# Attention's output by groups of 32 rows, and the state's update by heads, in a kernel of attention and two mixtures

## The chip, the core and the metric

The kernel runs on one core of one Trainium2 chip. The metric is the time of one execution on the device, in microseconds (us). A core has five engines that run at the same time, each through its own instructions in order: TensorE (PE in the profile; its loads of stationary operands are listed apart as PEld), VectorE (DVE), ScalarE (ACT), GpSimd (POOL) and SyncE (SP), which here issues most transfers. TensorE writes its products into PSUM, which has eight banks here.

## The reference

Three stages follow each other. The first is a recurrent attention over 768 steps, for 4 batches of 8 heads with 48 features each. The second is a mixture with a softmax gate on each hidden value over 3072 tokens of 384 features, and the third sends each token to one of 8 experts.

```python
for t in range(S):                       # attention: B, H, S, D = 4, 8, 768, 48
    cur = np.einsum('bhd,bhe->bhde', u[None] * kt, vt)
    y[:, :, t] = np.einsum('bhd,bhde->bhe', rt, state + cur)
    state = wt[:, :, :, None] * state + np.einsum('bhd,bhe->bhde', kt, vt)
x = attn_out.transpose(0, 2, 1, 3).reshape(B * S, H * D)
h = x @ w_in                             # 384 -> 1024
solu = h * softmax(h)
x = layernorm(solu) * g_ln @ w_out       # 1024 -> 384
e = argmax(x @ w_gate, axis=1)           # one of 8 experts for each token
out = gate * (relu(x @ w1[e]) @ w2[e])
```

## The kernel before

The 768 steps of a batch are cut into 6 chunks of 128, so that attention is 24 units of work (one chunk of one batch, 128 tokens by 384 features). In a unit the 8 heads form 4 pairs, p = 0 to 3, with q = 0 or 1 for the head in the pair. The state of a batch, `St[b]`, has for each pair 128 rows (64 for each head, 48 of them used) and 96 columns (48 for each head); blocks off the diagonal are zero.

A unit does this. TensorE transposes the inputs `lw`, `lr`, `lk` (line 693); DVE runs the decay's products along the chunk (line 709). The scores of each head (line 767) are products over 48 rows. They lie in rows 0 to 47 for q = 0 and 64 to 111 for q = 1, and go to bank 4 and bank 5; DVE copies them under the causal mask into `am` (line 771). Then comes the output, `y()`, at line 780. It is written transposed, features on the partitions, into bank 4: for each pair one product of the state's 96 columns with `rt` (none in a batch's first chunk), and for each head one product of 96 columns of `lv` with `am[:, q, p]`. In `lv` each head has 48 columns of values and 48 of zeros, so that a window of 96 columns puts a head's values into its half of the pair's 96 rows. The result has 96 partitions and 4 blocks of 128 tokens.

The mixture's weights are multiplied in three blocks of 128 features. So `high()` and `low()` (lines 785 to 793) copy the output into `xh` and `xl` as three blocks of 128 rows: rows 0 to 95 are pairs 0 to 2, and rows 96 to 127 hold a third of pair 3 each. That is four copies on ACT (line 785, and line 787 three times) and four subtractions on DVE (line 791, and line 793 three times). `x_rows` gives the rows of `w_in` the same order, which makes two transfers of each of the six loads of `w_in`.

The state's update multiplies the transposed keys `ks` (128 stationary columns of a pair) with the values of both heads (96 moving columns) at line 810; DVE adds the state (line 818) and POOL multiplies the diagonal blocks by the decay (line 823). In the middle stretch its product, the output and the scores of q = 0 share bank 4, one after the other.

All operands of lines 767, 780 and 810 are float32. Where the built program has one such product, the trace shows two instructions on PE; this text calls them passes. The mixture's products (lines 187 to 190) take operands split in two and are one instruction each.

The order is written out by hand. Each step has a nominal time, and a table of numbers says in which order the steps are issued; every engine keeps that order. First, attention runs beside the preparation of the mixture's weights (until some 116 us). Then attention's unit s runs beside the mixture's tile s - 7 (until some 376 us); the last seven tiles and the experts follow. Products that nobody reads (`warm`, line 1087) fill PE at some places of the first stretch.

Of the kernel before, what the change touches and what calls it, by code (L numbers as in the profile page):

```python
# [7 lines left out]
F32 = mybir.dt.float32  # L8
# [5 lines left out]
ALU = mybir.AluOpType  # L14
# [17 lines left out]
# Places by number of tokens, in the order in which they are worked on, and the room of each; the last one's rest has a path of its own.  # L32
# [5 lines left out]
# Issue order: position in the issue sequence -> index of the step in the plan sorted by nominal time.  # L38
# [82 lines left out]
def rwkv_moe_kernel(ctx: ExitStack, tc: tile.TileContext, r, k, v, w, u, w_in, w_out, g_ln, w_gate, w1, w2, out, dbg=None):  # L121
# [44 lines left out]
    # sums of the inverse decay products, of the squares of the first mixture, of the decay products: bounds that NaN fails too  # L166
# [16 lines left out]
    def mm3(o, terms):  # L183
        """The products of operands in two parts each, high parts first; the product of both low ones is below float32."""
        n = len(terms)
        for i, (ah, al, bh, bl) in enumerate(terms):
            nc.tensor.matmul(o, ah, bh, start=(i == 0), stop=False)  # L187
            nc.tensor.matmul(o, ah, bl, start=False, stop=False)  # L188
        for i, (ah, al, bh, bl) in enumerate(terms):
            nc.tensor.matmul(o, al, bh, start=False, stop=(i == n - 1))  # L190

    def mm3_steps(o, terms, n):
        """The same in pieces of n products."""
        seq = [(ah, b) for ah, al, bh, bl in terms for b in (bh, bl)] + [(al, bh) for ah, al, bh, bl in terms]
        for i, (a, b) in enumerate(seq):
            nc.tensor.matmul(o, a, b, start=(i == 0), stop=(i == len(seq) - 1))  # L196
            if i % n == n - 1:
                yield
# [5 lines left out]
    # A plan is a list of steps with nominal times; every engine issues its steps in that order.  # L204
# [11 lines left out]
    # The rows of a block of the attention's transpose: those of a pair of heads, and a third of the last pair's.  # L216
    def x_rows(kk):
        return (slice(0, 96), slice(96 * kk, 96 * kk + 96)), (slice(96, 128), slice(3 * 96 + 32 * kk, 3 * 96 + 32 * kk + 32))

    def from_f64(src, n, pool, ck=None):  # L220
        """float64 to float32 by its bits: sign and exponent and 20 bits of the high word, 3 of the low one.
        Below float32's range it is 0, or, with ck, sums there say that a value was below."""
# [21 lines left out]
    def prep_w_in(c, pool, ck=None):  # L244
        kk, n = divmod(c, 2)
        ns = slice(512 * n, 512 * n + 512)
        a = yield from from_f64([(rows, w_in[at, ns]) for rows, at in x_rows(kk)], 512, pool, ck)
        yield lambda: nc.scalar.copy(out=wih[:, kk, ns], in_=a)
        yield lambda: nc.gpsimd.tensor_tensor(out=wil[:, kk, ns], in0=a, in1=wih[:, kk, ns].bitcast(F32), op=ALU.subtract)
# [7 lines left out]
    def prep_gate(f, st, wgt, pool, tp, gp):  # L257
        """Rows of w_out times the gate's weights, for the logits to come out of the same product as the mixture."""
        def tr():
            for kk in range(KD):  # L260
                nc.tensor.transpose(tp[:, kk, :], st()[:, kk * 128:(kk + 1) * 128], ident)
        yield tr
        wT = pool("wT")[:, 0:DM].rearrange("p (k n) -> p k n", k=KD)
        yield lambda: nc.scalar.copy(out=wT, in_=tp)

        def lg():
            for kk in range(KD):
                nc.tensor.matmul(gp[:, f, :], wT[:, kk, :], wgt[:, kk, :], start=(kk == 0), stop=(kk == KD - 1))
        yield lg
# [43 lines left out]
    def moe_act(u, halves, mw):  # L313
        """halves: the hidden values, as one pattern or as two of one bank each."""
# [121 lines left out]
    def experts_loop(x2d=None, tokd=None):  # L436
        """Every expert over all tokens, the others' results dropped; without those over its sorted rows."""
# [56 lines left out]
    def general_path():  # L494
# [44 lines left out]
        with ExitStack() as gs:  # L539
# [11 lines left out]
            with tc.For_i(0, NTOK, 128) as t0:  # L551
                x = ga2.tile([128, DM], F32, tag="gx", name="gx")
                xk = x.rearrange("p (k n) -> p k n", k=KD)
                nc.sync.dma_start(out=xk[:, :, 0:96], in_=xd[bass.ds(t0, 128), 0:288].rearrange("p (k n) -> p k n", k=KD))
                nc.sync.dma_start(out=xk[:, :, 96:128], in_=xd[bass.ds(t0, 128), 288:384].rearrange("p (k n) -> p k n", k=KD))
# [20 lines left out]
    # the attention's buffers go when its last tile is done, and those of the experts take their room  # L576
# [23 lines left out]
    def xslot(m):  # L600
        """Where the two parts of a tile's transpose wait: in the first weight buffers, as long as no expert has them; one place apart, for the last tile."""
# [15 lines left out]
    def lazy(t, make, gaps):  # L617
        """Steps of a generator that allocates as it goes: each is drawn when its turn comes."""
# [10 lines left out]
    # Nominal times of the steps of a unit from the start of its step: attention with the preparation of  # L629
    # w_out beside it, with that of w_in, with a tile of the mixture, and the mixture alone.  # L630
# [122 lines left out]
    def plan_A(i, t, mode):  # L753
# [5 lines left out]
        yp = bank[4][0:2 * D]  # L759
# [15 lines left out]
        def y():  # L775
            vf = v_.rearrange("p h d -> p (h d)")
            terms = [(p, St[b][:, p, :], u["rt"][:, p, :]) for p in range(4)] if c else []
            terms += [(p, vf[:, 96 * (2 * p + q) - 48 * q:96 * (2 * p + q) - 48 * q + 96], u["am"][:, q, p, :]) for q in range(2) for p in range(4)]
            for n, (p, a, m) in enumerate(terms):
                nc.tensor.matmul(yp[:, p, :], a, m, start=(n == 0), stop=(n == len(terms) - 1), skip_group_check=True)  # L780
# [3 lines left out]
        def high():  # L784
            nc.scalar.copy(out=xh[0:96], in_=yp[:, 0:3, :])
            for kk in range(KD):
                nc.scalar.copy(out=xh[96:128, kk, :], in_=yp[32 * kk:32 * kk + 32, 3, :])
        at(o("x"), high)

        def low():  # L790
            nc.vector.tensor_tensor(out=xl[0:96], in0=yp[:, 0:3, :], in1=xh[0:96].bitcast(F32), op=ALU.subtract)
            for kk in range(KD):
                nc.vector.tensor_tensor(out=xl[96:128, kk, :], in0=yp[32 * kk:32 * kk + 32, 3, :], in1=xh[96:128, kk, :].bitcast(F32), op=ALU.subtract)
# [14 lines left out]
        def mm():  # L808
            for p in range(4):
                nc.tensor.matmul(up[:, p, :].rearrange("p (q d) -> p q d", q=2), u["ks"][:, p, :], v_[:, 2 * p:2 * p + 2, 0:D], start=True, stop=True)  # L810
# [40 lines left out]
    # groups of token tiles that are gated together  # L851
# [44 lines left out]
    def gate_steps(g, bk):  # L896
        """The first of the largest logits' experts, its gate, the row among the sorted tokens, and the way there."""
# [69 lines left out]
    # The first is the one with most of the first tokens, so that its work can start before the last tokens have theirs;  # L967
    # the others follow by their numbers of tokens, as PLACE has it. The j-th has room for SLOTS[j] tokens.
# [90 lines left out]
    # the first loads, then the constant buffers  # L1059
# [8 lines left out]
    def init():  # L1068
# [10 lines left out]
        # each partition's sums start at its share of the expert's first row: ranks come out as rows  # L1079
# [4 lines left out]
    def warm(n):  # L1084
        """The tensor engine's clock rises only under load: products that nobody reads, where there is no work yet."""
# [21 lines left out]
    def scratch(c):  # L1107
        """Where the preparation of a block of weights works: buffers that the mixture uses later."""
# [12 lines left out]
    def named(make, times):  # L1121
        """Steps of a generator at given times."""
# [80 lines left out]
    def check():  # L1203
        """1 for more tokens of the last place, 2 for a place with too little room, 4 for decays or values out of bounds or an expert's rows overrun."""
# [79 lines left out]
    # the first expert's first tokens, beside the end of the first mixture  # L1284
# [18 lines left out]
    # the order of the others  # L1303
# [18 lines left out]
    for j in range(1, NE):  # L1322
        # the weights and tokens of a place are made ready during the one before
# [72 lines left out]
```

## Time and profile before

| | |
|---|---|
| median of 3 runs | 702.67 us (701.42, 702.67, 703.84) |
| profiled execution, from its first to its last instruction | 701.8 us |
| PE busy | 650.1 us (93%), 4279 instructions |
| DVE, ACT, POOL busy | 444.6, 346.1, 350.8 us |
| mean granted clock of PE | 0.972 of 2.4 GHz |

For the profiled execution the page gives the span alone; its own time on the device is not listed apart from the three runs. A matmul's end is modelled in the profile, so that matmuls in a row overlap on paper: how long one occupies PE is read from the distance between starts. A "busy" PE can therefore be waiting for its own pipeline.

### The profile page before, as it was taken

The page shows a single profiled execution, that of the slowest core. Times are in us where ns is not written, and L with a number is a line of the kernel's source. Part 1 is how long each engine was busy: PE and PEld are TensorE (multiplying, and loading weights), DVE is VectorE, ACT ScalarE, POOL GpSimd, SP SyncE. Part 2 cuts the span into 40 slices and gives each one's busy share as a digit, 9 for nine tenths or more (in the row PEclk, how much of TensorE's full clock was granted, in tenths as well). Part 3 has the DMA queues.
Part 4 walks back from the last instruction along what each step waited for, and adds up shares of the span by engine and source line. Part 5 has one row for each costly group of instructions (what it writes and reads, how often), then busy time and mean ns, then how long its engine had stood idle before and what let it go on. Part 6 is the DMA issues. An engine that isn't in the chain of part 4 may idle for free. (4 is left out here: it accounts for less than half of the span.)

```text
span 701.8 us, 11888 instructions
## 1 busy us (share of the span) xinstructions
PE 650.1 (93%) x4279; PEld 604.1 (86%) x4279; DVE 444.6 (63%) x947; ACT 346.1 (49%) x759; POOL 350.8 (50%) x341
## 2 busy tenths in 40 slices
PE   6787779898999999999989999999999999999993
PEld 6777668887988978998978998999899999999993
DVE  7999999968987888699887779752203121131220
ACT  3677566545553545545643556433535344353430
POOL 5666578344344445344461153326637374667721
PEclk9789799999999999999999999999999999999997
DMA  7856323562611413050200420155444253544400
GB/s 175 210 132 146 95 59 90 170 170 58 147 35 33 104 23 68 23 114 24 57 35 13 154 84 13 57 160 188 149 141 139 91 176 125 182 135 145 157 20 35
DMA packets 125193, 72.45 MB, mean 103 GB/s; under 512 B 104167, under 2 KB 115932, under 8 KB 125125
## 3 DMA queue, kind: packets, MB, share of 16 engines
q1 hardware_dynamic: 121845, 62.13, 33.3%
q0 software_dynamic: 3280, 9.47, 3.6%
q8 instruction: 36, 0.59, 0.4%
q14 instruction: 32, 0.26, 0.1%
HBM read 55.79 MB, written 16.29 MB: 103 GB/s over the span
## 5 line engine op out<-in xcount | busy, mean ns | idle before, releaser
L1257 DVE SCALAR_TENSOR_TENSOR hl<-bank,hh 128x384 fp32r<-128x384 f32 (+5 forms) x70 | 37.6, 552 | 141.4 <-ACT hh L1256 125.8
L1050 POOL TENSOR_TENSOR wbl<-stg,wbh 128x768 fp32r<-128x768 f32 x32 | 58.8, 1852 | 30.0 <-ACT wbh L1049 25.6
L196 PE MATMUL bank<-wbh,hh 128*128 128x384 f32 (+4 forms) x216 | 72.9, 338 | 0.0
L196 PE MATMUL bank<-wbl,hh 128*128 128x384 f32 (+4 forms) x216 | 72.6, 336 | 0.0
L187 PE MATMUL bank<-xth,wah 128*128 128x384 f32 (+5 forms) x210 | 71.2, 345 | 0.5 <-DVE rr L955 0.5
L1050 POOL TENSOR_TENSOR wal<-stg,wah 128x1024 fp32r<-128x1024 f32 x24 | 57.3, 2401 | 28.1 <-ACT wah L1049 28.1
L188 PE MATMUL bank<-xtl,wah 128*128 128x384 f32 (+5 forms) x210 | 69.7, 337 | 0.0
L187 PE MATMUL bank<-wbh,lh 128*128 128x392 f32 x192 | 67.5, 351 | 1.3 <-ACT xo L873 0.8
L1256 ACT ACTIVATE hh<-bank 128x384 fp32r<-128x384 f32 (+5 forms) x70 | 33.6, 490 | 66.6 <-PE bank L190 59.0
L188 PE MATMUL bank<-wbl,lh 128*128 128x392 f32 x192 | 65.5, 341 | 0.0
L748 POOL TENSOR_TENSOR am<-ident,a 128x1024 f32<-128x1024 f32 x24 | 46.7, 1946 | 28.0 <-DVE a L743 19.8
L1276 POOL DMA_INDIRECT out_dram<-yo,xg x28 | 27.6, 984 | 64.6 <-ACT yo L1273 42.7
L726 POOL TENSOR_TENSOR tq<-qe,yq 128x512 f32<-128x512 f32 x24 | 29.7, 1238 | 60.0 <-ACT yq L721 59.9
L780 PE MATMUL bank<-am,lv 128*96 128x128 f32 x384 | 49.3, 284 | 5.7 <-DVE am L771 4.8
L780 PEld LDWEIGHTS bank<-am,lv 128*96 128x96 f32 x384 | 45.9, 171 | 6.7 <-DVE am L771 3.2
L823 POOL TENSOR_TENSOR St<-su,qe 64x192 f32<-64x192 f32 x40 | 24.8, 621 | 48.0 <-DVE su L818 36.4
L190 PE MATMUL bank<-xth,wal 128*128 128x384 f32 (+5 forms) x210 | 48.2, 337 | 0.0
L961 POOL DMA_INDIRECT xsd<-xo,ai x24 | 25.4, 1057 | 35.0 <-DMA xsd<-xo,ai 14.1
L187 PE MATMUL pair<-wah,wah 128*128 128x512 f32 x102 | 42.1, 413 | 0.0
L196 PE MATMUL bank<-wbh,hl 128*128 128x384 f32 (+4 forms) x216 | 42.1, 336 | 0.0
L187 PEld LDWEIGHTS bank<-xth,wah 128*128 128x128 f32 x210 | 39.5, 188 | 2.3 <-DVE rr L955 0.7
L188 PEld LDWEIGHTS bank<-xtl,wah 128*128 128x128 f32 x210 | 39.5, 188 | 1.3
(241 smaller groups left out, 1753.0 us busy)
## 6 DMA issues: line engine op xcount, KB each, us to landing
stg<-in_moe_w_dram SPq DMA_DIRECT2D x32, 384.0 KB, 4.5
stg<-in_moe_w_dram SPq DMA_DIRECT2D x24, 512.0 KB, 4.5
xsd<-zrow SPq DMA_DIRECT2D x16, 386.0 KB, 3.8
xg<-xsd SPq DMA_DIRECT2D x24, 193.0 KB, 2.7
lw<-in_w_dram SPq DMA_DIRECT2D x24, 192.0 KB, 3.3
lr<-in_r_dram SPq DMA_DIRECT2D x24, 192.0 KB, 4.2
lk<-in_k_dram SPq DMA_DIRECT2D x24, 192.0 KB, 3.8
lv<-in_v_dram SPq DMA_DIRECT2D x24, 192.0 KB, 3.1
```

The costliest lines, as they stand in the source:

```text
L187: nc.tensor.matmul(o, ah, bh, start=(i == 0), stop=False)
L188: nc.tensor.matmul(o, ah, bl, start=False, stop=False)
L190: nc.tensor.matmul(o, al, bh, start=False, stop=(i == n - 1))
L196: nc.tensor.matmul(o, a, b, start=(i == 0), stop=(i == len(seq) - 1))
L726: nc.gpsimd.tensor_tensor(out=u["tq"], in0=u["qe"][:, :, 1:129], in1=u["yq"], op=ALU.mult)
L748: nc.gpsimd.tensor_tensor(out=u["am"].rearrange("p q a t -> p (q a) t"), in0=ident.rearrange("p (o t) -> p o t", o=1).to_broadcast([128, H ...
L780: nc.tensor.matmul(yp[:, p, :], a, m, start=(n == 0), stop=(n == len(terms) - 1), skip_group_check=True)
L961: nc.gpsimd.indirect_dma_start(out=xsd, out_offset=bass.IndirectOffsetOnAxis(ap=u["ai"][:, j, :], axis=0), in_=MU[m]["xo"], in_offset=None ...
L1050: at(t + c1, lambda: eng.tensor_tensor(out=dl(), in0=u["st"], in1=dh().bitcast(F32), op=ALU.subtract))
L1256: at(t + d1, lambda: nc.scalar.activation(out=P2["h", 0][:, f, cs], in_=hp, func=AF.Relu))
L1257: at(t + d2, lambda: nc.vector.scalar_tensor_tensor(out=P2["h", 1][:, f, cs], in0=hp, scalar=0.0, in1=P2["h", 0][:, f, cs].bitcast(F32), o ...
L1276: nc.gpsimd.indirect_dma_start(out=out, out_offset=bass.IndirectOffsetOnAxis(ap=xg(j, i)[0:n, XW - 1:XW].bitcast(I32), axis=0), in_=box["y ...
```

## The change

The output's block for a pair, 96 rows, is cut into three groups of 32 rows; group g = 3p + j goes to partitions 32 (g mod 4) and block g div 4. The 12 groups fill three blocks of 128 partitions, in the order in which the features come. A product has 32 stationary columns and writes 32 partitions. A group takes one product with the state (unless the chunk is the first) and one with `am`, or two where a group has columns of both heads (j = 1). Consecutive products go to different groups of 32 partitions. `high` and `low` become one copy and one subtraction of 128 rows, `x_rows` goes, and each load of `w_in` is one transfer. The update multiplies 64 stationary columns of one head with that head's 48 moving columns; the blocks off the diagonal are not written any more. The steps and the table of their order stay as they are; the rest of the diff removes comments, which moves line numbers (780 becomes 779, 810 becomes 806).

```diff
-        a = yield from from_f64([(rows, w_in[at, ns]) for rows, at in x_rows(kk)], 512, pool, ck)
+        a = yield from from_f64([(slice(0, 128), w_in[kk * 128:(kk + 1) * 128, ns])], 512, pool, ck)
...
-        yp = bank[4][0:2 * D]
+        yp = bank[4]
...
         def y():
             vf = v_.rearrange("p h d -> p (h d)")
-            terms = [(p, St[b][:, p, :], u["rt"][:, p, :]) for p in range(4)] if c else []
-            terms += [(p, vf[:, 96 * (2 * p + q) - 48 * q:96 * (2 * p + q) - 48 * q + 96], u["am"][:, q, p, :]) for q in range(2) for p in range(4)]
-            for n, (p, a, m) in enumerate(terms):
-                nc.tensor.matmul(yp[:, p, :], a, m, start=(n == 0), stop=(n == len(terms) - 1), skip_group_check=True)
+            st = [(3 * p + j, St[b][:, p, 32 * j:32 * j + 32], u["rt"][:, p, :]) for p in range(4) for j in range(3)] if c else []
+            one = lambda j, q, off: [(3 * p + j, vf[:, 96 * (2 * p + q) + off:96 * (2 * p + q) + off + 32], u["am"][:, q, p, :]) for p in range(4)]
+            terms = st + one(0, 0, 0) + one(1, 0, 32) + one(1, 1, -16) + one(2, 1, 16)
+            begun = set()
+            for n, (g, a, m) in enumerate(terms):
+                kk, i = divmod(g, 4)
+                nc.tensor.matmul(yp[32 * i:32 * i + 32, kk, :], a, m, start=i not in begun, stop=n == len(terms) - 1, skip_group_check=True)
+                begun.add(i)
...
-        def high():
-            nc.scalar.copy(out=xh[0:96], in_=yp[:, 0:3, :])
-            for kk in range(KD):
-                nc.scalar.copy(out=xh[96:128, kk, :], in_=yp[32 * kk:32 * kk + 32, 3, :])
-        at(o("x"), high)
+        at(o("x"), lambda: nc.scalar.copy(out=xh, in_=yp[:, 0:KD, :]))
 
         def low():
-            nc.vector.tensor_tensor(out=xl[0:96], in0=yp[:, 0:3, :], in1=xh[0:96].bitcast(F32), op=ALU.subtract)
-            for kk in range(KD):
-                nc.vector.tensor_tensor(out=xl[96:128, kk, :], in0=yp[32 * kk:32 * kk + 32, 3, :], in1=xh[96:128, kk, :].bitcast(F32), op=ALU.subtract)
+            nc.vector.tensor_tensor(out=xl, in0=yp[:, 0:KD, :], in1=xh.bitcast(F32), op=ALU.subtract)
...
             for p in range(4):
-                nc.tensor.matmul(up[:, p, :].rearrange("p (q d) -> p q d", q=2), u["ks"][:, p, :], v_[:, 2 * p:2 * p + 2, 0:D], start=True, stop=True)
+                for q in range(2):
+                    rows = slice(64 * q, 64 * q + 64)
+                    nc.tensor.matmul(up[rows, p, D * q:D * q + D], u["ks"][:, p, rows], v_[:, 2 * p + q, 0:D], start=True, stop=True)
```

On PE, at the output of a unit in the middle stretch, the program before has these rows (bank_161 is bank 4; a size is that of what is written):

```order
L693 MATMUL bank_164<-ident,lk_172 128x128 x4
L693 MATMUL bank_160<-ident,lw_166 128x128 x4
L780 MATMUL bank_161<-rt,St_180 96x128 x4
L780 MATMUL bank_161<-am,lv_174 96x128 x8
L388 MATMUL bank_162<-ident,cc 128x128 x4
L388 MATMUL bank_160<-ident,cc 128x128 x4
```

and the changed one has these in the same place:

```order
L687 MATMUL bank_164<-ident,lk_172 128x128 x4
L687 MATMUL bank_160<-ident,lw_166 128x128 x4
L779 MATMUL bank_161<-rt,St_180 32x128 x12
L779 MATMUL bank_161<-am,lv_174 32x128 x16
L384 MATMUL bank_162<-ident,cc 128x128 x4
L384 MATMUL bank_160<-ident,cc 128x128 x4
```

Twelve products of 96 columns have become 28 of 32 columns; what stands ahead of them and behind them is the same.

On PE, at the state's update that stands behind a mixture's tile, before:

```order
L190 MATMUL bank_159<-wbh_129,ll 128x392 x8
L810 MATMUL bank_161<-lv_176,ks 128x96 x4
L693 MATMUL bank_163<-ident,lr_169 128x128 x4
L800 MATMUL bank_160<-ident,kt 128x128 x4
L767 MATMUL bank_161<-rt,kt 128x128
```

and changed:

```order
L190 MATMUL bank_159<-wbh_129,ll 128x392 x8
L806 MATMUL bank_161<-lv_176,ks 64x48 x8
L687 MATMUL bank_163<-ident,lr_169 128x128 x4
L794 MATMUL bank_160<-ident,kt 128x128 x4
L761 MATMUL bank_161<-rt,kt 128x128
```

Four products have become eight smaller ones, in place.

On DVE, in the middle stretch, the subtractions that take the output out of bank 4 (`wal_126`, the first weight buffers, is where a tile's `xl` waits), before:

```order
L347 TENSOR_SCALAR rs<-sep 128x1
L348 RECIPROCAL rs<-rs 128x1
L791 TENSOR_TENSOR wal_126<-bank_161,wah_125 96x384
L793 TENSOR_TENSOR wal_126<-bank_161,wah_125 32x128 x3
L743 TENSOR_REDUCE a_3309<-ru 128x4x2
L728 SCALAR_TENSOR_TENSOR tq<-tq,yq 128x512
```

and changed:

```order
L343 TENSOR_SCALAR rs<-sep 128x1
L344 RECIPROCAL rs<-rs 128x1
L787 TENSOR_TENSOR wal_126<-bank_161,wah_125 128x384
L737 TENSOR_REDUCE a_3537<-ru 128x4x2
L722 SCALAR_TENSOR_TENSOR tq<-tq,yq 128x512
```

Four instructions have become one; their neighbours stay in their order.

## Rows read from the trace of the kernel before

**Rows 1.** The page: span, then busy time, share and instructions of each engine.

```profile
span 701.8 us, 11888 instructions
...
PE 650.1 (93%) x4279; PEld 604.1 (86%) x4279; DVE 444.6 (63%) x947; ACT 346.1 (49%) x759; POOL 350.8 (50%) x341
```

**Rows 2.** Busy time by stretch: length, busy time of each engine, clock, DMA.

```profile
core 0: us, PE busy (x) PEld busy (x) DVE busy (x) ACT busy (x) POOL busy (x), PEclk, DMA share, GB/s
...
20.00:100.00 80.00, 59.73 (x482) 55.72 (x481) 78.41 (x105) 53.51 (x131) 52.26 (x44) 0.84 0.51 121
...
116.00:376.00 260.00, 247.42 (x1756) 225.29 (x1755) 219.76 (x461) 131.89 (x311) 114.19 (x130) 1.00 0.29 72
```

**Rows 3.** Waits of PE from 116 to 376 us: total, times, longest.

```profile
PE bank L780 <- DVE am L771: 4.0, 4, 1.9
...
PE bank L810 <- DVE wal L793: 0.9, 1, 0.9
```

**Rows 4.** Timeline of PE: start, duration, engine, line, tiles, sizes, count.

```profile
262.00 0.60 PE L693 MATMUL bank<-ident,lk 128*128 128x128 f32 x4
262.44 0.60 PE L388 MATMUL bank<-ident,cc 128*128 128x128 f32 x4
263.81 1.11 PE L780 MATMUL bank<-rt,St 128*96 128x128 f32 x8 [0.77 <-DVE am L771]
264.76 1.91 PE L780 MATMUL bank<-am,lv 128*96 128x128 f32 x16
266.51 0.60 PE L388 MATMUL bank<-ident,cc 128*128 128x128 f32 x4
...
271.09 1.03 PE L810 MATMUL bank<-lv,ks 128*128 128x96 f32 x8
271.95 0.60 PE L693 MATMUL bank<-ident,lk 128*128 128x128 f32 x4
```

**Rows 5.** Line 780 from 116 to 376 us: count, min/median/max ns, starts.

```profile
L780 PEld LDWEIGHTS bank<-am,lv x256: 159/163/163, 132.3 to 375.7; 128*96 128x96 f32 x128
L780 PE MATMUL bank<-am,lv x256: 272/273/317, 132.4 to 375.8; 128*96 128x128 f32 x128
...
L780 PE MATMUL bank<-rt,St x128: 272/273/350, 131.5 to 374.0; 128*96 128x128 f32 x128
```

**Rows 6.** Line 810 in the same stretch.

```profile
L810 PE MATMUL bank<-lv,ks x104: 243/275/350, 116.0 to 321.3; 128*128 128x96 f32 x104
```

**Rows 7.** Timeline of PE around the scores of line 767.

```profile
277.12 0.60 PE L693 MATMUL bank<-ident,lw 128*128 128x128 f32 x4
277.65 1.16 PE L767 MATMUL bank<-rt,kt 48*128 48x128 f32 x16
278.75 0.66 PE L388 MATMUL bank<-ident,cc 128*128 128x128 f32 x4
279.24 0.60 PE L693 MATMUL bank<-ident,lr 128*128 128x128 f32 x4
```

**Rows 8.** Line 767 alone by stretch: PE's instructions touching it, in brackets.

```profile
277.64:277.76 0.12, 0.11 (x2) 1.00 0.00 0
277.76:277.90 0.14, 0.14 (x4) 1.00 0.00 0
```

**Rows 9.** Timeline of DVE: the copies of one unit's output.

```profile
268.90 0.54 DVE L791 TENSOR_TENSOR xs<-bank,xs 96x384 fp32r<-96x384 f32 x1
269.45 0.89 DVE L793 TENSOR_TENSOR xs<-bank,xs 32x128 fp32r<-32x128 f32 x3
```

**Rows 10.** Line 1250: copies of 128x384 from PSUM on DVE.

```profile
L1250 DVE TENSOR_TENSOR xtl<-bank,xth x16: 497/548/559, 467.8 to 656.1; 128x384 fp32r<-128x384 f32 x15, 128x336 fp32r<-128x336 f32 x1
```

**Rows 11.** Line 791 from 20 to 100 us.

```profile
L791 DVE TENSOR_TENSOR wal<-bank,wah x5: 523/540/543, 25.7 to 88.2; 96x384 fp32r<-96x384 f32 x5
L791 DVE TENSOR_TENSOR xs<-bank,xs x1: 547/547/547, 49.4 to 49.4; 96x384 fp32r<-96x384 f32 x1
```

**Rows 12.** All waits of DVE from 20 to 100 us.

```profile
DVE am L771 <- PE bank L767: 0.5, 1, 0.5
```

More of the change, by code (lines that the diff above doesn't have):

```diff
@@ L214, in rwkv_moe_kernel @@
     woh, wol = WB[1]
-    def x_rows(kk):
-        return (slice(0, 96), slice(96 * kk, 96 * kk + 96)), (slice(96, 128), slice(3 * 96 + 32 * kk, 3 * 96 + 32 * kk + 32))
     def from_f64(src, n, pool, ck=None):
@@ L552, in general_path @@
                 x = ga2.tile([128, DM], F32, tag="gx", name="gx")
-                xk = x.rearrange("p (k n) -> p k n", k=KD)
-                nc.sync.dma_start(out=xk[:, :, 0:96], in_=xd[bass.ds(t0, 128), 0:288].rearrange("p (k n) -> p k n", k=KD))
-                nc.sync.dma_start(out=xk[:, :, 96:128], in_=xd[bass.ds(t0, 128), 288:384].rearrange("p (k n) -> p k n", k=KD))
+                nc.sync.dma_start(out=x, in_=xd[bass.ds(t0, 128), :])
                 xx, rstd = general_moe1(x, gmw, gpst, gph, gpx)
```

## The prediction

> **What bounds the kernel now.** I read the page's engine line first, then busy time by stretch, then the waits of the two busiest engines, then the timeline of one unit. The page names PE as the busiest engine, 93% of a span of 701.8 us [rows 1]. That is an average over stages, so the stretches count. From 20 to 100 us, where attention runs beside the preparation of weights, DVE is busy 78.41 of 80 us and PE only 59.73 [rows 2]; DVE waits there for 0.5 us in all [rows 12]. DVE sets that pace. From 116 to 376 us, where attention runs beside the mixture, PE is busy 247.42 of 260 us at a granted clock of 1.00 and DVE 219.76 [rows 2]. The largest wait of PE there adds up to 4.0 us [rows 3]. PE sets that pace, with some 5% of slack. The change touches attention alone, so what comes after 376 us only shifts.
>
> The order on every engine stays, and no step is moved past another. So a cheaper instruction can only bring forward what hangs on it, and a dearer one delay it. The question is what the new products cost on PE, in a middle stretch that holds 16 outputs: 256 passes with `am` at 16 a unit, 128 with the state at 8 a unit [rows 5]. It holds 13 updates: 104 passes at 8 a unit [rows 6].
>
> **The output on PE.** Before, 16 passes take from 264.76 to 266.51 us [rows 4], 0.109 us each, so the 24 of a unit take 2.62 us. After, 28 products make 56 passes, each with 128 moving columns as now. The trace of before has no product on a part of the columns. Its nearest rows are the scores, products on a part of the rows: 16 passes with the same 128 moving columns take from 277.65 to 278.75 us [rows 7], 0.069 each, against 0.109 on the whole array. The stretches show why: two passes are running by 277.76, and two more have begun by 277.90 [rows 8]. Two halves of the array work side by side, two passes about every 0.11 us. If four groups of 32 columns do the same, 56 passes are 14 rounds of 0.109 us, 1.53 us.
>
> Going over to a part of the array and back has its price. The four transposes ahead of the scores take 0.53 us until the first score (277.12 to 277.65), where four transposes inside a run take 0.44 (262.00 to 262.44): 0.09 more. The scores take 1.10 us where 8 rounds would be 0.87: 0.23 more. The four transposes behind them take 0.49 (278.75 to 279.24): 0.05 more [rows 4, 7]. That is 0.37 us each time. So the output costs 1.53 + 0.37 = 1.90 us, 0.72 less than 2.62. The price can be near nothing where PE had been waiting before the output, as at 263.81 [rows 4], and twice as much at worst: a gain of 1.09 to 0.35 us a unit. I take 0.72, since most outputs follow other work directly. Times 16 units: 11.5 us, with bounds of 17.4 and 5.6.
>
> A rule of the Trainium skill speaks against this. TensorE: Matmul & The Clock Gate, Part 3, says that a weight load overlaps running matmuls only when the row groups differ, and groups of columns share all their rows. Here the trace disagrees for the whole array: the loads of line 780 last 163 ns each, and passes still start every 109 ns [rows 4, 5]. By the rule the load would stand ahead of each round, 14 x 0.27 = 3.8 us an output, and slower; I don't use it.
>
> **The update on PE.** Before, 8 passes take 0.86 us (271.09 to 271.95) [rows 4]. After, 16 passes go to two halves of the columns, 8 rounds. A round lasts as long as the larger of its parts: 48 moving columns at 0.109/128 us each are 0.041 us; half of the 0.108 us that a pass with 128 stationary columns takes here is 0.054. With 0.37 for going over that is 0.80, 0.06 less. Bounds: the rounds don't shrink (8 x 0.108 + 0.37 = 1.23, 0.37 more), or going over is free and the moving columns decide (0.33, 0.53 less). Over 13 units I take 0.8 us of gain, between 4.8 us of loss and 6.9 of gain.
>
> **The copies out of bank 4.** On DVE, one subtraction of 0.54 and three of 0.89 us together [rows 9] become one of 128x384; the experts' copies of that size take 0.548 [rows 10]. That is 0.88 us less in each unit. From 20 to 100 us six units do it [rows 11], where DVE sets the pace: 5.3 us. I take 5.0, since the freed time can end in a wait for POOL or a transfer; the bounds are 7.0 (all eight units ahead of 116 us) and 2.5 (half goes into waits). In the middle stretch DVE has 40 us to spare [rows 2], and its part there is only that PE waits less behind it: 0.9 us for line 793 [rows 3], taken as nothing. ACT's four copies become one as well; ACT is busy 131.89 of 260 us there [rows 2] and hides either form. The six transfers of `w_in` that are no longer doubled count as nothing: neither DVE nor PE waits for one in these rows.
>
> **What is queued behind.** No wait is added: the output waits for the state, then for the diagonal from POOL, then for the second mask, at the same places as before. The second half of the output waits for the second mask; behind it on PE stand transposes or the mixture's products, which wait as they do now.
>
> **The sum.** The middle stretch: 11.5 + 0.8 = 12.3 us, of which I count 85%, because PE will now wait a little more often for DVE's masks (4.0 us today [rows 3]): 10.4. The first stretch: 5.0. Together 15.4, which makes a span of 686.4. The runs' median, 702.67, lies 0.9 us above the span of 701.8 [rows 1]; with that the forecast is 687 us. With the bounds above, the likeliest case reaches from 674 (17.4 + 6.9 + 7.0, less some slack) to 698 (5.6 of gain for the output, 4.8 of loss for the update, 5.0 for DVE, less slack).
>
> **The rivals.**
>
> Two at a time (9%, slower). The trace shows two passes side by side; nothing in it shows four. The two passes of one float32 product go to the same group of columns and must follow each other. If PE starts passes strictly in order, the second pass of a product holds up the next product's first, and just about two run at once. Then the output is 28 rounds, 3.05 + 0.37 = 3.42 us, 0.80 more than now; 16 of these are 12.8 us, less 5.0 from DVE: 710.5 us. It decides as soon as fewer than about 2.5 passes run at once, where 56 passes cost what 24 do now. Against it: the scores are pairs of passes too, and two are under way from the first 0.12 us [rows 8]; with a product's second pass held in order, the first would be alone there. The same Part 3 states that rule, matmuls strictly first in, first out; by it this rival would be the forecast. It says as well that groups of columns overlap nearly as well as groups of rows, which no row here shows.
>
> No overlap at all between groups of columns (5%, far slower). The output is 56 x 0.109 + 0.37 = 6.47 us, 3.85 more, 62 us in the middle stretch; the update 16 x 0.054 + 0.37 = 1.23, 0.37 more, 5 us. In the first stretch PE's growth eats DVE's gain. About 769 us.
>
> Another engine takes over (10%). PE gets lighter by 12 us in 260, and DVE's busy time of 219.76 falls by 14. If the order by hand makes PE wait for masks, scans and copies at new places, half of the gain in the middle stretch goes: 702.67 - 6.2 - 4 = 692.5. For it: the waits for line 771 come in four places already [rows 3]. Against it: DVE keeps its 40 us of room.
>
> Going over costs much more with columns (4%): each entry and exit near 1.1 us instead of 0.37 cancels the output's gain, and the update's loss, 13 x 0.7, takes DVE's gain and more: about 703 us, no change.
>
> **How the numbers follow.** The forecast has 72%, the rivals 9, 5, 10 and 4. What a measurement of this kernel tells from no change is about 0.3%, 2.1 us. Faster by more than that: the forecast and the engine that takes over, less 2% for their edges, 80%. Within it: the costly switch and a little more, 5%. Slower: the first two rivals and an edge, 15%. The range of 674 to 704 holds nearly all of the first case, the engine that takes over and the costly switch, some 8 in 10; it leaves out the two slower rivals and the gains beyond all bounds.
>
> **What would show it.** Right: line 779's 56 passes take about 1.6 us from the first to the last start, four under way at a time, with 0.1 us more at either end; the middle stretch from about 116 to 376 us shortens by some 10 us; line 787 takes 0.55 us; the mixture's first products start some 5 us earlier. Wrong: an output of 3 us or more (two at a time) or 6 (none); the transposes behind an output late by more than 0.5 us; or an output of 1.9 us with PE's idle time grown, the waits for line 765 (the masks) above all. A lower granted clock in the middle stretch than 1.00 would be something that I have not counted.

## The result, and the profile after

The changed kernel takes 686.02 us (median of 4 runs, 684.15 to 689.47), against 702.83 us for the kernel before (4 runs beside them, 701.42 to 703.84): a ratio of 0.9768, 95% interval 0.9738 to 0.9797. The forecast was 687 us. The number came out; where it came from was only half right, and the experiments below are about that.

The page of the changed kernel: span, then busy time, share and instructions of each engine, as in [rows 1].

```profile
span 685.1 us, 13436 instructions
...
PE 636.9 (93%) x5143; PEld 576.3 (84%) x5143; DVE 418.1 (61%) x875; ACT 325.4 (47%) x687; POOL 349.7 (51%) x341
```

PE has 864 more passes and 13.2 us less busy time, DVE 26.5 us less. The output, by the timeline of PE (columns as in [rows 4]); the passes that follow it are transposes:

```profile
254.76 0.86 PE L779 MATMUL bank<-rt,St 128*32 128x128 f32 x24 [0.26 <-DVE am L765]
255.44 1.06 PE L779 MATMUL bank<-am,lv 128*32 128x128 f32 x32
256.43 0.66 PE L384 MATMUL bank<-ident,cc 128*128 128x128 f32 x4
```

56 passes from 254.76 to 256.43 are 1.67 us, where 24 took 2.70 (263.81 to 266.51) [rows 4]. Of the 15 outputs from 127 to 345 us, 13 take 1.46 or 1.47 us from the first start to the last, as this one does; the other two take 1.93 and 1.98. Line 779 alone, by stretch (PE's and PEld's instructions that touch the stretch in brackets; columns as in [rows 8]):

```profile
254.75:254.80 0.05, 0.04 (x4) 0.04 (x6) 1.00 0.17 35
254.80:254.95 0.15, 0.15 (x8) 0.15 (x12) 1.00 0.45 95
```

Four passes are under way by 254.80, and four more have begun by 254.95: four at a time. The update, by the timeline of PE of the same kernel:

```profile
245.95 0.67 PE L806 MATMUL bank<-lv,ks 128*64 128x48 f32 x16
246.55 0.66 PE L794 MATMUL bank<-ident,kt 128*128 128x128 f32 x4
```

The subtraction on DVE, by its source line (count, min/median/max ns, starts):

```profile
L787 DVE TENSOR_TENSOR wal<-bank,wah x20: 524/547/560, 25.5 to 348.0; 128x384 fp32r<-128x384 f32 x20
```

The update takes 0.60 us against 0.86 [rows 4], line 787 takes 0.547 us where lines 791 and 793 took 1.43 [rows 9]. Busy time by stretch, of the kernel before in a stretch that has no row above (columns as in [rows 2]):

```profile
112.00:360.00 248.00, 235.42 (x1664) 213.97 (x1663) 210.75 (x432) 127.97 (x301) 113.73 (x129) 1.00 0.30 73
```

The same view of the changed kernel:

```profile
20.00:100.00 80.00, 66.12 (x715) 55.97 (x714) 72.95 (x94) 49.15 (x115) 54.52 (x48) 0.69 0.50 127
112.00:360.00 248.00, 233.31 (x2373) 202.52 (x2373) 205.36 (x417) 119.31 (x267) 114.00 (x129) 0.99 0.31 75
```

In the first stretch DVE now has 7 us of idle time in 80 where it had 1.6 [rows 2]. In the middle PE sits idle for 14.7 us of 248, before for 12.6: it works nearly as densely as before, on less work. The scan on DVE (line 703, before 709) runs once a unit, so its starts tell where the time was won: that of unit 8 and that of unit 23 bound the middle stretch.

| kernel | scan of unit 8 | of unit 23 | between | span |
|---|---|---|---|---|
| before | 111.4 | 350.4 | 239.0 | 701.8 |
| changed | 107.7 | 334.8 | 227.1 | 685.1 |
| split copies | 109.4 | 346.0 | 236.6 | 697.6 |
| slow output | 106.5 | 341.3 | 234.8 | 693.1 |
| DVE filler | 119.3 | 360.2 | 240.9 | 717.0 |

(us, from the profiled runs, one execution each; the last three are experiments.) The change wins 3.7 us ahead of unit 8, 11.9 in the middle and 1.1 behind it. The middle repeats well: three executions whose middle holds the same work (the changed kernel and both kernels on the clock below) have it at 227.1, 226.5 and 226.7 us.

### The profile page after: what moved, and what is told of

It is laid out like the page before. It is cut to its first block, busy times and chain, and to the rows that moved or that the text cites. A ratio compares the mean times of both kernels' runs of the same rounds, so it can differ in the third digit from the quotient of the medians.

```text
span 685.1 us, 13436 instructions
## 1 busy us (share of the span) xinstructions
PE 636.9 (93%) x5143; PEld 576.3 (84%) x5143; DVE 418.1 (61%) x875; ACT 325.4 (47%) x687; POOL 349.7 (51%) x341
## 5 line engine op out<-in xcount | busy, mean ns | idle before, releaser
L765 DVE COPY_PREDICATED am<-causal,bank 128x512 f32<-128x512 int32 x48 | 34.2, 737 | 13.2 <-PE bank L761 8.7
L188 PE MATMUL pair<-wal,wah 128*128 128x512 f32 x102 | 40.9, 401 | 0.0
```

What stands on the lines that cost most here:

```text
L765: nc.vector.copy_predicated(out=u["am"][:, q], mask=causal.bitcast(I32).rearrange("p (o t) -> p o t", o=1).to_broadcast([128, 4, 128]), da ...
```

## The experiments

Each starts from the changed kernel unless it says otherwise. Ratios are to the kernel before, run beside it; the ratio of the changed kernel is 0.9768 [0.9738, 0.9797].

**Which half pays: the products without the copies.** The output's copies are in four parts again, on ACT and DVE, with the new products.

```diff
-            nc.vector.tensor_tensor(out=xl, in0=yp[:, 0:KD, :], in1=xh.bitcast(F32), op=ALU.subtract)
+            nc.vector.tensor_tensor(out=xl[0:96], in0=yp[0:96, 0:KD, :], in1=xh[0:96].bitcast(F32), op=ALU.subtract)
+            for kk in range(KD):
+                nc.vector.tensor_tensor(out=xl[96:128, kk, :], in0=yp[96:128, kk, :], in1=xh[96:128, kk, :].bitcast(F32), op=ALU.subtract)
```

(the same for `high` on ACT)

> The changed kernel with the output's copies in four parts again (rows 0 to 95, then rows 96 to 127 three times), products as changed. Theory (DVE sets the pace of the first stretch, PE of the middle one): DVE does 0.88 us more in each unit; the start of the middle stretch comes some 4 us later than in the changed kernel, the middle stretch is longer by less than 2 us: 690 to 692 us. Rival A (the copies held up PE in the middle stretch too, and the output's products brought little): some 14 us more there, 700 us or above. Rival B (copies are hidden everywhere): no change, 686 us.

Measured: 699.43 us, ratio 0.995 [0.9936, 0.9963]. Without the copies 13.4 us are gone, four fifths of the gain. Busy time by stretch:

```profile
112.00:360.00 248.00, 227.80 (x2276) 197.88 (x2275) 210.05 (x438) 127.36 (x309) 113.78 (x130) 0.98 0.30 75
```

PE's work fell and PE's idle time grew: 20.2 us of 248, where the kernel before had 12.6. The cheaper products turned into waiting. The same from the scan of unit 8 to that of unit 23, in the kernel before, the changed one and this one:

```profile
111.40:350.40 239.00, 228.34 (x1614) 207.69 (x1613) 203.18 (x418) 125.71 (x296) 108.20 (x123) 1.00 0.31 76
107.70:334.80 227.10, 214.51 (x2163) 186.24 (x2162) 189.45 (x373) 111.74 (x250) 107.26 (x122) 0.99 0.33 80
109.40:346.00 236.60, 218.72 (x2165) 189.91 (x2164) 200.96 (x418) 121.88 (x293) 107.82 (x123) 0.98 0.31 77
```

Idle time is 10.7, 12.6 and 17.9 us. The 9.5 us between the last two rows are 5.3 us of idle time and 4.2 us in which PE is busy longer with the same work, at a lower mean clock. Here is one such place: by the timeline of PE a wait for DVE, and by busy time the stretch behind it, in which PE is busy throughout at the clock's lower level:

```profile
168.27 0.66 PE L687 MATMUL bank<-ident,lk 128*128 128x128 f32 x4 [1.54 <-DVE kt L726]
169.10:176.00 6.90, 6.90 (x35) 6.41 (x34) 4.99 (x11) 4.86 (x10) 4.56 (x5) 0.51 0.51 113
```

So a part of what the split copies cost is PE's clock; that the wait brought it down was not tried. By the waits of PE from 112 to 360 us (total, times, longest), the waiting is behind DVE:

```profile
PE bank L779 <- DVE am L765: 4.3, 5, 2.2
PE bank L384 <- DVE cc L359: 2.0, 2, 1.3
...
PE bank L687 <- DVE kt L726: 1.8, 2, 1.5
...
PE bank L800 <- DVE kt L726: 1.4, 2, 0.7
...
PE bank L812 <- DVE wal L793: 1.2, 2, 0.7
```

**The same with ACT's copy alone in four parts** (`high` as above, `low` in one).

> The changed kernel with ACT's copy of the output in four parts again and DVE's subtraction in one. Theory D (DVE's own time is what the split costs): near the changed kernel, 686 to 688 us. Theory L (the length of the chain from output to free bank counts, whichever engine adds to it; ACT's four copies are 0.8 us longer than one, DVE's four 0.9): about half of the 13.4 us of the split, 691 to 694 us.

Measured: 686.79 us, 0.979 [0.9762, 0.9818]: no difference that can be told from the changed kernel. From the scan of unit 8 to that of unit 23 it takes 228.9 us (104.7 to 333.6), with 10.1 us more of busy time on ACT. So it is DVE's subtraction that the split copies paid for.

**The copies without the products.** 20 unread products a unit (16 in a first chunk) go to a free part of the bank, which lengthens the output to what it was:

```diff
-            terms = st + one(0, 0, 0) + one(1, 0, 32) + one(1, 1, -16) + one(2, 1, 16)
+            idle = lambda n: [(12 + j % 4, ident[:, 0:32], u["rt"][:, 0, :]) for j in range(n)]
+            terms = (st + idle(4) if c else []) + one(0, 0, 0) + one(1, 0, 32) + idle(8) + one(1, 1, -16) + one(2, 1, 16) + idle(8)
```

> The changed kernel with products that nobody reads added to each output (20 of 32 columns into the free block of bank 4, 16 in a batch's first chunk), so that an output takes PE some 2.7 us again, as before the change; copies and update as changed. With the split copies (699.4 us, so the products alone bring 3.8 us) it fills a table of two by two. Theory C (the copies alone carry the gain, DVE sets the pace of the middle stretch too): 686 to 689 us. Theory B (two chains of equal length: either part alone brings little, both together the 17 us): 696 to 701 us. Theory P (PE's microseconds count one by one, the prediction's sum): 16 times 1.0 us more, 701 to 703 us. The order with runs of one group, an output of 2.4 us at 689.0 us in all, speaks for C or for something between C and B, some 690 to 693 us.

Measured: 693.7 us, 0.9879 [0.9854, 0.9904]. One output, by the timeline of PE, from its first passes to the transposes behind it:

```profile
256.01 0.86 PE L780 MATMUL bank<-rt,St 128*32 128x128 f32 x24 [0.64 <-DVE am L765]
...
258.77 0.66 PE L384 MATMUL bank<-ident,cc 128*128 128x128 f32 x4
```

From the first to the last start an output now takes 2.56 us (1.46 in the changed kernel), and PE is the fuller engine:

```profile
112.00:360.00 248.00, 239.78 (x2883) 211.12 (x2880) 198.81 (x394) 117.02 (x262) 114.84 (x130) 1.00 0.31 76
```

With these, products alone give 0.5%, copies alone 1.2%, both together 2.3%: more than their sum. Each alone is partly eaten by the engine that was not relieved, the products alone by a lower clock as well.

**Is it DVE's time or the late output?** Four unread subtractions a unit on DVE, behind line 787, so that the output's low part is as early as in the changed kernel and only DVE's queue is longer.

```diff
+    unread = const.tile([128, 128], F32, name="unread")
...
             nc.vector.tensor_tensor(out=xl, in0=yp[:, 0:KD, :], in1=xh.bitcast(F32), op=ALU.subtract)
+            for _ in range(4):
+                nc.vector.tensor_tensor(out=unread[96:128], in0=xh[96:128, 0, :].bitcast(F32), in1=ident[96:128], op=ALU.subtract)
```

> The changed kernel, with four unread subtractions of 32x128 (operands in SBUF, result never read) on DVE in each of the 24 units, directly behind the subtraction of line 787. DVE's queue gets some 0.8 to 1.0 us more per unit, about what the split copies took (0.88), but the low part of the output is ready as early as in the changed kernel, its bank comes free as early, and no other engine waits for the new instructions. If DVE's time in its queue is what the split copies cost (every step behind them on DVE comes later), this is as slow as the split copies were: ratio about 0.995 (699 us), slower than the changed kernel by 10 to 13 us. If the late output itself cost the time (what reads the low part or its bank), and DVE's queue has room, it stays at 0.977 to 0.980 (686 to 688.5 us). In between, both take part, in that share.

Measured: 715.92 us, 1.0186 [1.0167, 1.0205], slower than either theory had it, because the filler was larger than meant. The groups of line 790 (busy us, mean ns, idle before):

```profile
L790 DVE TENSOR_TENSOR unread<-wah,ident 32x128 f32<-32x128 f32 x80 | 40.3, 504 | 2.6
...
L790 DVE TENSOR_TENSOR unread<-xs,ident 32x128 f32<-32x128 f32 x16 | 4.8, 298 | 0.5
```

The larger of them by source line (min/median/max ns, starts):

```profile
L790 DVE TENSOR_TENSOR unread<-wah,ident x80: 286/289/2437, 26.1 to 377.0; 32x128 f32<-32x128 f32 x80
```

The filler held DVE for 45.1 us in all instead of some 20 to 24. Per microsecond it agrees with the split copies: 29.9 us slower for 45.1 us of DVE is 0.66; 13.4 us slower for 24 x 0.88 = 21.1 us is 0.64. The late output is not needed to explain the split copies; DVE's time in its queue is enough. And DVE is not full, by the busy time from 112 to 360 us:

```profile
112.00:360.00 248.00, 222.18 (x2254) 191.71 (x2253) 216.59 (x444) 117.21 (x260) 113.24 (x129) 0.99 0.33 79
```

216.59 us of 248, 31 us idle, and each microsecond more still delays the kernel by two thirds of one. Line 790 alone, between the scans of units 8 and 23 (the busy time is DVE's):

```profile
119.30:360.20 240.90, 21.83 (x60) 0.99 0.31 75
```

That is the price's denominator in the table further down. All engines in the same stretch:

```profile
119.30:360.20 240.90, 216.84 (x2167) 187.31 (x2166) 209.77 (x433) 112.00 (x251) 107.21 (x122) 0.99 0.31 75
```

POOL is busy for 107.2 us, as in the changed kernel: the filler did not make POOL's own instructions longer. From 112 to 360 us PE's idle time is now 25.8 us, again behind DVE (the two largest waits of PE there):

```profile
PE bank L797 <- DVE kt L727: 6.4, 6, 2.0
PE bank L780 <- DVE am L766: 4.5, 5, 1.4
```

**The order of the products.** Within each segment the products are sorted by group of 32 columns, so that neighbours share one.

```diff
-            terms = st + one(0, 0, 0) + one(1, 0, 32) + one(1, 1, -16) + one(2, 1, 16)
+            by = lambda ts: sorted(ts, key=lambda t: t[0] % 4)
+            terms = by(st) + by(one(0, 0, 0) + one(1, 0, 32)) + by(one(1, 1, -16) + one(2, 1, 16))
```

> The changed kernel with its 28 products of an output in another order: between the same waits, all products of one group of 32 columns stand together (three of the state, then two, then two), so that neighbours share their columns. Theory Q (PE keeps the groups' passes apart and looks past a group that is busy): an output stays near 1.7 us and the kernel at 686 us. Theory F (passes start strictly in order): the passes of a run follow each other, only the border of two runs overlaps, some 45 rounds of 0.109 us, 4.9 us an output: 16 times 3.2 us more in the middle stretch and some in the first, 735 to 750 us. Between: it looks past a few instructions only, 2.5 to 4 us an output, 700 to 720 us.

Measured: 689.0 us, 0.9791 [0.9775, 0.9807]. One output, by the timeline of PE:

```profile
253.17 1.26 PE L780 MATMUL bank<-rt,St 128*32 128x128 f32 x20 [0.26 <-DVE am L765]
254.16 0.31 PE L780 MATMUL bank<-am,lv 128*32 128x128 f32 x2
254.23 0.30 PE L780 MATMUL bank<-rt,St 128*32 128x128 f32 x2
254.29 0.32 PE L780 MATMUL bank<-am,lv 128*32 128x128 f32 x3
254.37 0.27 PE L780 MATMUL bank<-rt,St 128*32 128x128 f32 x1
254.40 0.32 PE L780 MATMUL bank<-am,lv 128*32 128x128 f32 x3
254.48 0.27 PE L780 MATMUL bank<-rt,St 128*32 128x128 f32 x1
254.51 1.11 PE L780 MATMUL bank<-am,lv 128*32 128x128 f32 x24
255.56 0.66 PE L384 MATMUL bank<-ident,cc 128*128 128x128 f32 x4
```

All 24 passes with the state (`rt,St`) stand ahead of those with `am` in the program, yet `am` passes start from 254.16 while state passes still start at 254.48. By these rows a pass whose group was free went past passes that waited for a busy one. So an output takes 2.39 us, between 1.67 and the 6.1 of 56 passes one by one. Those 0.72 us more, 11.5 us of PE in the middle's 16 outputs, cost the kernel some 3; between the scans of units 8 and 23 it takes 231.2 us (105.0 to 336.2).

**The update.** The old products in the changed kernel, and the new ones in the kernel before.

```diff
-                for q in range(2):
-                    rows = slice(64 * q, 64 * q + 64)
-                    nc.tensor.matmul(up[rows, p, D * q:D * q + D], u["ks"][:, p, rows], v_[:, 2 * p + q, 0:D], start=True, stop=True)
+                nc.tensor.matmul(up[:, p, :].rearrange("p (q d) -> p q d", q=2), u["ks"][:, p, :], v_[:, 2 * p:2 * p + 2, 0:D], start=True, stop=True)
```

> The changed kernel with the update as before (128 stationary, 96 moving columns). The trace of the changed kernel shows the update at 0.60 us where it was 0.86. Theory (every PE microsecond in the middle stretch counts): 13 updates times 0.26 us, 3.4 us slower than the changed kernel, 689.4 us. Rival (the update stands where PE waits anyway, as the prediction's small term had it): within 1 us of the changed kernel, 686 to 687 us.

> The kernel before with only the update changed to 64 stationary and 48 moving columns for each head. Theory: 13 times 0.26 us on a PE that sets the pace, 699.4 us against 702.8. Rival: no change, 702 to 703 us.

Measured: 688.03 us, 0.9784 [0.9766, 0.9803], with the old update; 702.89 us, 0.9996 [0.9982, 1.001], with the new one alone. The first cannot be told from the changed kernel (the medians lie 2.0 us apart, and the intervals allow 3.5), the second is no change. Between the scans of units 8 and 23 the old update makes the changed kernel 3.1 us longer (104.6 to 334.8), the new one makes the kernel before 0.7 us shorter (109.4 to 347.7). So 0.26 us on PE, 13 times in the middle, is worth up to some 3 us beside the other changes and nothing that shows without them.

**The clock in the first stretch.** The changed kernel's granted clock from 20 to 100 us is 0.69 in the mean, between its levels of 1.2 and 2.4 GHz; before it was 0.84 [rows 2]. One kernel adds 20 unread products ahead of the scores of units 1 to 6, the other leaves out all unread products of line 1083.

```diff
+            if 1 <= i < 7:
+                warm(20)
```

```diff
-    WARM = (28, -213.38, 17, 35.27, 40, -60.18, 7, -131.3, 21, 14.69, 0, 23.63, 11, 143.22, 1, 178.42)
+    WARM = (0, -213.38, 0, 35.27, 0, -60.18, 0, -131.3, 0, 14.69, 0, 23.63, 0, 143.22, 0, 178.42)
```

> The changed kernel with 20 products that nobody reads ahead of the scores of six units in the first stretch, where PE often waits. In the profile of the changed kernel PE ran at the lower clock for 55 of the first 112 us, in the one before for 31, and the first stretch gained 4.1 us; in the one with the old update it ran there at the lower clock for 34 us and the stretch gained 6.8. Theory (the lower clock eats part of DVE's gain): some 2 us faster than the changed kernel, 684 us, with less time at the lower clock. Rival (the clock is not what counts there, and the added products delay the scores): 686 to 689 us.

> The changed kernel without any of the products that nobody reads. Theory (the clock of the first stretch costs time): more of the first 112 us at the lower clock than 55, and 2 to 4 us slower than the changed kernel, 688 to 690 us. Rival (DVE sets the pace whatever PE's clock): within 1 us of 686 us.

Measured: 687.47 us, 0.9793 [0.9769, 0.9818], with 20 products more; 685.57 us, 0.9762 [0.9737, 0.9788], with none. Busy time and clock from 20 to 100 us with more of them:

```profile
20.00:100.00 80.00, 62.01 (x831) 54.05 (x828) 75.30 (x93) 49.40 (x115) 54.59 (x48) 0.85 0.51 127
```

The same with none:

```profile
20.00:100.00 80.00, 63.04 (x699) 53.71 (x697) 73.94 (x95) 49.55 (x115) 57.12 (x49) 0.77 0.52 130
```

The clock is 0.85 and 0.77, and neither time can be told from the changed kernel's; the unread products aren't needed. That the clock costs nothing there is not shown: the scan of unit 8 starts at 107.1 and 105.0 us in these two, at 104.6 (clock 0.81) with the old update and at 107.7 in the changed kernel, so a cost of up to some 3 us stays possible.

**Work taken off DVE.** The centring of the mixture's activations (line 359, 0.75 us on DVE at the median) goes to ACT: in the changed kernel, in the kernel before, and in the changed kernel without unread products.

```diff
-            nc.vector.tensor_scalar(out=u["cc"], in0=u["s"], scalar1=u["nmu"], scalar2=None, op0=ALU.add)
+            nc.scalar.activation(out=u["cc"], in_=u["s"], func=AF.Identity, bias=u["nmu"])
```

> The changed kernel with the centring of the mixture's hidden values (cc = s - mean, 128x1024, 0.92 us on DVE in each of 24 tiles) moved to ACT, which is busy less than half of the time; the same numbers are computed. So far the split of DVE's subtraction costs some 11 us, ACT's split 1 to 2 and a slow output on PE 8. Theory D (DVE's own time paces most of the middle stretch): 16 tiles there by 0.92 us, of which six tenths count as they did for the split copies: 7 to 10 us faster than the changed kernel, 676 to 679 us. Theory L (what counts is the length of the chain through bank 4, not DVE's load): no gain, 685 to 688 us, or slower where the centring waits behind ACT's other work.

> The kernel before with the centring on ACT and nothing else. Theory D: DVE paces the middle stretch of the kernel before as well, 6 to 12 us faster than before, 691 to 697 us. Theory P (PE alone paced it, as the prediction said): no change, 702 us.

> The changed kernel with the centring on ACT and without the products that nobody reads. Without them alone the changed kernel stayed where it was (0.9762 of the kernel before, against 0.9768). Expected within 1 us of the run with the centring on ACT, 676 to 679 us if theory D holds.

Measured: 698.68 us, 0.993 [0.9914, 0.9946]; 720.72 us, 1.0245 [1.0225, 1.0266]; 699.0 us, 0.9944 [0.9931, 0.9958]. All are slower than what they started from, by 13 to 18 us, although DVE has less to do. On ACT the step takes 1.15 us, and ACT waits for its input with everything behind it (waits from 112 to 360 us):

```profile
ACT cc L359 <- DVE nmu L357: 23.0, 10, 5.6
...
PEld bank L384 <- ACT cc L359: 5.6, 4, 3.2
```

So this doesn't measure DVE's time alone: it puts a hand-over between two engines into the mixture's chain, and that costs more than DVE's 0.75 us gives. As a test of DVE's load it failed; the filler above is the cleaner one.

## Why the prediction was right, and where it was wrong

**The output: right, a little better.** 1.67 us. The forecast of 1.90 held 0.14 for the transposes on either side, so 1.76 stands against it. A round of four passes lasts 0.11 us: in the run with the slow output, 40 passes more took 1.10. Going over, within the output, was sized at 0.23 and is about 0.14 (1.67 less 14 x 0.109). Both slower rivals fell with this row, and the costly switch too. The sum of that one was wrong besides: by its own terms, 702.67 + 9.1 - 5.0, it is 706.8 us and not 703.

**The update: mechanism right, size off.** 0.60 us, forecast 0.80. Its term in the sum was 0.8 us; by the two experiments it is between nothing and some 3.

**The first stretch: about right.** 5.0 us forecast, 3.7 measured up to unit 8, in one execution each; by the spread of unit 8's scan given with the clock it could be 2 to 7. DVE waits there now, for the scores, POOL and ACT, where it waited 0.5 us in all [rows 12]; the waits of DVE from 20 to 100 us:

```profile
DVE am L765 <- PE bank L761: 3.6, 3, 1.9
DVE am L765 <- POOL am L742: 1.8, 1, 1.8
DVE wal L787 <- ACT wah L784: 1.0, 1, 1.0
```

**The middle stretch: the sum right (10.4 forecast, 11.9 measured), its reason wrong.** The step that failed is the one that reads the middle stretch as PE's alone: "PE sets that pace", "DVE has 40 us to spare", and so the copies' 0.88 us a unit "taken as nothing". Between the scans of units 8 and 23 lie 15 units. There the runs give these prices:

| taken from the changed kernel | engine time added | slower by | per us |
|---|---|---|---|
| split copies, DVE | 15 x 0.88 = 13.2 | 236.6 - 227.1 = 9.5 | 0.72 |
| filler, DVE | 21.8 (line 790's busy time there) | 240.9 - 227.1 = 13.8 | 0.63 |
| slow output, PE | 15 x 1.10 = 16.5 | 234.8 - 227.1 = 7.7 | 0.47 |
| sorted products, PE | 15 x 0.72 = 10.8 | 231.2 - 227.1 = 4.1 | 0.38 |
| ACT's copy in four, ACT | 10.1 (busy time) | 228.9 - 227.1 = 1.8 | 0.18 |

The middle's spread of 0.6 us makes these good to about 0.1. The first row holds the 4.2 us at a lower clock. These are slopes at the changed kernel and don't add up to the 11.9.

The prediction had PE's microsecond at 0.85 and DVE's at 0. Both errors nearly cancelled, and that they did was luck. What the profile showed and I passed over: every wait of PE named in [rows 3] is for DVE, and so are 11.5 of the 12.3 us in that view as a whole. An engine that is 95% busy and spends nearly all of the rest waiting for one other engine is not the pace by itself. The two take turns (scores on PE, masks on DVE, output on PE, subtraction, scan and time shift on DVE, transposes on PE), in an order fixed by hand; DVE's idle time lies at places where its next instruction isn't ready. They are not alone in it. The waits of DVE in the changed kernel from 112 to 360 us, the largest for each of three engines:

```profile
DVE su L814 <- PE bank L806: 4.8, 6, 1.1
DVE tq L722 <- POOL tq L720: 4.8, 5, 1.4
DVE rs L343 <- ACT e L337: 4.7, 7, 1.3
```

In all DVE waits some 14 us for PE, 13 for ACT and 9 for POOL. So time added to PE or DVE is paid in part, and time taken from one alone turns in part into waits for the other: products alone shortened the middle by 2.4 us, copies alone by 4.2, both by 11.9. What the rival "another engine takes over" describes is what the products alone show, and in the changed kernel the copies' gain paid for it.

**On the strict order.** The rival with two passes at a time is what follows from the Trainium skill, TensorE: Matmul & The Clock Gate, Part 3, which has matmuls start and end strictly in program order. The run with sorted products disagrees: a later `am` pass starts at 254.16, ahead of state passes at 254.48. The measurement decides. In the changed kernel neighbours go to different groups, and the order costs nothing there.

**Left open.** I can't name one chain of instructions for the whole middle stretch. That PE and DVE both count, and by how much, is shown; that the price is paid at the waits listed is read from the rows and was not tried wait by wait. POOL's part has no price: no run adds to it or takes from it.

## What to carry to other kernels

A busy share of 95% didn't make PE the bound here, and 85% didn't make DVE free: look at what ends the idle time of the fullest engine, and if it is nearly always the same other engine, price both. The quickest price is a filler: unread work of known length in one engine's queue, and the slope of the kernel's time by it; read the filler's length from the trace, since here it came out at twice what was meant. A change that relieves both ends of such a chain can be worth more than its halves measured alone, as here, so a half that measures as nothing should not be dropped before it is tried with the other.

## What the runs showed of the hardware

- Groups of 32 columns work side by side, four passes every 0.11 us at a clock of 1.00 (40 passes more took 1.10 us in the slow output). With sorted products, passes of one group start ahead of earlier ones of another (254.16 and 254.48); neighbours in one group made an output 0.72 us longer, not four times as long.
- A subtraction of 32x128 on DVE with both operands in SBUF took 0.286 us, but up to 2.44 us (line 790 above), while the subtractions of the same size that read PSUM stayed between 0.285 and 0.298 us in the run with split copies. Of the 96, 21 last over 0.32 us, and POOL is at work for at least 69% of each of these; 59 of the other 75 have no operation of POOL beside them. DVE's timeline around 92.6 us in the run with the filler:

```profile
92.62 4.43 DVE L790 TENSOR_TENSOR unread<-wah,ident 32x128 f32<-32x128 f32 x4
```

POOL's timeline there:

```profile
92.68 1.27 POOL L246 TENSOR_TENSOR wal<-a,wah 128x512 fp32r<-128x512 f32 x1
93.92 0.99 POOL L732 TENSOR_TENSOR ru<-lr,ub 128x384 f32<-128x384 f32 x1
94.99 1.00 POOL L733 TENSOR_TENSOR ru<-ru,lk 128x384 f32<-128x384 f32 x1
```

Four subtractions take 4.43 us, and until 96.0 us POOL works beside them with gaps under 0.1 us; the first of the four alone takes the 2.44. The Trainium skill, SBUF — State Buffer, section "SBUF: two separate sides", says that an operation of DVE with two SBUF inputs and one of GpSimd that reads SBUF take the same ports as an exclusive lock for the whole instruction; these rows agree.
- A mean clock of 0.69, 0.85 or 0.77 between 20 and 100 us in three kernels made no difference in their times that can be told. In the middle, PE's work between two scans took 218.7 us at a mean clock of 0.98 and 214.5 at 0.99.
